# The stores of x in the attention, issued by SyncE behind a step's loads instead of by ScalarE

## The chip, the cores and the metric

The kernel runs on one core of one Trainium2 chip. The metric is the device time of one execution in microseconds. A core has five engines that run side by side, each with an instruction queue of its own: TensorE (PE; its weight loads are shown as PEld), VectorE (DVE), ScalarE (ACT), GpSimd (POOL) and SyncE (SP), which here only issues DMAs and waits. DMAs can be issued from the queues of SyncE, ScalarE and GpSimd, and are carried out by 16 DMA engines of the core.

## The reference

A recurrent attention block (4 batches, 8 heads, 768 positions, head size 48) is followed by a mixture of 8 experts, in which every expert gets exactly 384 of the 3072 rows.

```python
f = 1.0 / (1.0 + np.exp(-f_logit))
for t in range(S):
    state = f[:, :, t, :, None] * state + np.einsum('bhd,bhe->bhde', k[:, :, t], v[:, :, t])
    y[:, :, t] = np.einsum('bhd,bhde->bhe', q[:, :, t], state)
x = y.transpose(0, 2, 1, 3).reshape(B * S, H * D)          # 3072 x 384
logits = x @ w_gate                                        # 3072 x 8
# the best free (row, expert) pair first; every expert takes N / E = 384 rows: assigned[row]
for e in range(E):
    out[assigned == e] = np.maximum(x[assigned == e] @ w1[e], 0.0) @ w2[e]
```

## The kernel before

The attention is cut into 24 chunks: 6 stretches of 128 positions for each of the 4 batches, all 8 heads of a chunk at once. A chunk passes through stages, and the stages of several chunks are run beside each other: in step s, the stage with number n works on chunk s - n. There are 29 steps. The order of the stages in a step is written out by hand (lists `FILLING` for the first 6 steps, `FULL`, `LAST`), and the scheduler keeps that order on TensorE, VectorE, ScalarE and GpSimd. SyncE is not in that list: the order of its DMAs is the scheduler's, which takes them as it expects them to become possible.

What happens to a chunk, with the names that the text uses:

- `load` (L169, SyncE): f of the chunk three steps ahead, then q, k and v of the chunk two steps ahead, at the head of each step. Each is 192 KB, read as 1024 runs of 192 bytes. f has three buffers, q and k four, v seven; a load waits until its buffer's last reader is done.
- `clamp` (L175, GpSimd), the last but two in a step, on the chunk of the next step; `decays` (L180, L181, ScalarE): exp and log of f give g.
- `split` (L191 VectorE `upper`, L193 GpSimd `low`, L199 ScalarE `high`), then `sums` (L210, TensorE): running sums L of g.
- `factors` (L221 VectorE `dl`, L223 and L224 ScalarE `eq`, `ek`), and q and k times these: `gated_q` (L240), `gated_k` (L246, GpSimd).
- `halves` and `span` (L235, L250, L254 GpSimd, L256 ScalarE `gl`), `decayed` (L289, GpSimd R), `added` (L299) and `new_state` (L311): the state that goes on to the batch's next chunk.
- `q_columns` and `k_columns` (L264 TensorE, L272 ScalarE `qT`, L279 VectorE `kT`): transposes.
- `scores` (L322 TensorE A, L327 VectorE `am`), `values` (L337) and `queries` (L351): the chunk's rows of x in PSUM (Y). In `queries` ScalarE copies them to the tile x in SBUF (L358, two copies) and, before the change, issues the store of x to `xd` in HBM (L361). x has three buffers.
- `transposed` (L370, TensorE X), `x_copy` (L382, VectorE), `gate` (L390), `to_logits` (L400): the logits of the chunk, from the x in SBUF.

In a step of `FULL`, `queries` (stage 4) is the last but one: ScalarE copies and stores the x of chunk s - 4 at the step's end, and the first thing in its queue behind that is `decays` of the next step. TensorE starts the next step with `transposed` of the same x. The scratch array `xd` is read much later: the gather of an expert's rows (L1034, GpSimd) takes rows of it by number.

After the attention the experts' rows are found by counting, and expert after expert is computed, while the next expert's rows are found.

Every DMA that SyncE or ScalarE issues counts up one of eight completion semaphores, which are handed round in the order that the scheduler gives the DMAs; before one is used again, the issuing engine waits until the DMA that had it before has landed. That wait is an instruction in the issuing engine's queue.

Of the kernel before, what the change touches and what calls it, by code (L numbers as in the profile page):

```python
# [27 lines left out]
def kernel(  # L28
# [32 lines left out]
    nc = tc.nc  # L61
# [5 lines left out]
    C = 128  # L67
# [31 lines left out]
    xd = dram.tile([N + 32, D], FP32, name="xd")  # L99
# [243 lines left out]
    def queries(G):  # L343
        b, c, Y = G["b"], G["c"], G["Y"]
        G["x"] = x = work.tile([128, D], FP32, name="x", tag="x", bufs=3)
        if G["R"] is not None:
            for hp in range(HP):
                for j in range(2):
                    for par in range(2):
                        rows = slice(DP * par, DP * par + DH)  # L350
                        nc.tensor.matmul(  # L351
                            out=Y[par][HC * j:HC * j + HC, DH * hp:DH * hp + DH],
                            lhsT=G["qT"][rows, hp, HC * j:HC * j + HC],
                            rhs=G["R"][rows, hp, :],
                            start=False, stop=True, skip_group_check=True)
        for par in range(2):
            copy = nc.vector.tensor_copy if par and last(G) else nc.scalar.copy
            copy(out=x[:].rearrange("t (a r d) -> t r a d", r=2, d=DH)[:, par],  # L358
                 in_=Y[par][:, 0:HP * DH].rearrange("t (a d) -> t a d", d=DH))
        row = S * b + C * c  # L360
        nc.scalar.dma_start(out=xd[row:row + C, :], in_=x[:])  # L361

    def last(G):
        return G.get("i") == len(chunks) - 1
# [41 lines left out]
    def beside(G):  # L406
# [11 lines left out]
                        (added, 2), (values, 4), (halves, 1), (gate, 5), (gated_q, 1),  # L418
                        (new_state, 2), (decays, 0), (gated_k, 1), (span, 1), (to_logits, 5),
                        (split, 0), (beside, 0), (clamp, -1), (queries, 4), (split_high, 0),  # L420
                        (scores, 3)))
    FULL = ((decayed, 2), (decays, 0), (transposed, 5), (sums, 1), (added, 2), (x_copy, 5),
            (factors, 1), (split, 0), (split_high, 0), (k_copy, 3), (halves, 1), (new_state, 2),
            (values, 4), (span, 1), (gate, 5), (gated_q, 1), (gated_k, 1), (to_logits, 5),
            (q_columns, 2), (k_columns, 2), (k_last, 2), (beside, 0), (clamp, -1), (queries, 4),
            (scores, 3))
    LAST = ((scores, 3),) + FIRST + ((x_copy, 5), (k_copy, 2), (values, 4), (queries, 4),
                                     (gate, 5), (to_logits, 5), (counts_so_far, 5),
                                     (beside, 5))
# [59 lines left out]
    def ramp(n, name, step, base, when=later):  # L489
# [18 lines left out]
          in_=in_group[:].unsqueeze(2).to_broadcast((128, CG, E)))  # L508
# [813 lines left out]
    with tc.If(again[0] > 0):  # L1322
# [9 lines left out]
        with tc.For_i(0, B, 1) as b:  # L1332
            x = pool.tile([128, NCH, D], FP32, name="xb", tag="xb", bufs=1)
            with tc.For_i(0, HP, 1) as hp:
                scan_pair(pool, x, b, hp)
            nc.sync.dma_start(
                out=xd[0:N, :].rearrange("(b c t) d -> b t c d", b=B, c=NCH)[
                    bass.ds(b, 1)].rearrange("b t c d -> (b t) c d"),
                in_=x[:])
# [12 lines left out]
        out=outs[NT - 1][:, :],  # L1352
        out_offset=bass.IndirectOffsetOnAxis(ap=last_token[:, TE - 1:TE], axis=0),
        in_=o[:], in_offset=None, bounds_check=N - 1, oob_is_err=False)
# [29 lines left out]
```

## Time and profile before

| | |
|---|---|
| median of 9 runs | 452.08 us (449.57 to 454.69) |
| the profiled execution | 451.56 us |
| its span, first to last instruction | 449.6 us |
| granted TensorE clock, mean | 0.977 of full speed |
| TensorE busy | 428.4 us, 95% |
| VectorE busy | 274.5 us, 61% |
| ScalarE busy | 128.7 us, 29% |
| GpSimd busy | 175.1 us, 39% |
| loads of f, q, k and v | 24 each, 192 KB, 5.1, 4.5, 4.8 and 4.8 us from issue to landing (medians) |
| stores of x | 24, 192 KB, 3.1 us from issue to landing, first at 23.8 us, last at 151.9 us |
| DMA queue q10 | 3504 packets, 4.77 MB, 3.0% of the span of 16 engines |

In the lines of the profile, L361 is line 361 of the kernel, `out<-in` are the kernel's names of tiles, and "x24" is a count. In a timeline the first column is the start in microseconds from the first instruction, the second the length; what stands in brackets is how long the engine had been idle before, and what ended that. ACTq and SPq are the sequencers of ScalarE and SyncE, where a DMA's issue shows. The rows of 40 digits give the busy share in tenths for 40 equal slices of the span.

### The profile page before, as it was taken

The page shows a single profiled execution, that of the slowest core. Times are in us where ns is not written, and L with a number is a line of the kernel's source. Part 1 is how long each engine was busy: PE and PEld are TensorE (multiplying, and loading weights), DVE is VectorE, ACT ScalarE, POOL GpSimd, SP SyncE. Part 2 cuts the span into 40 slices and gives each one's busy share as a digit, 9 for nine tenths or more (in the row PEclk, how much of TensorE's full clock was granted, in tenths as well). Part 3 has the DMA queues.
Part 4 walks back from the last instruction along what each step waited for, and adds up shares of the span by engine and source line. Part 5 has one row for each costly group of instructions (what it writes and reads, how often), then busy time and mean ns, then how long its engine had stood idle before and what let it go on. Part 6 is the DMA issues. An engine that isn't in the chain of part 4 may idle for free. (4 is left out here: it accounts for less than half of the span.)

```text
span 449.6 us, 11815 instructions
## 1 busy us (share of the span) xinstructions
PE 428.4 (95%) x4830; PEld 288.3 (64%) x4830; DVE 274.5 (61%) x879; ACT 128.7 (29%) x302; POOL 175.1 (39%) x231
## 2 busy tenths in 40 slices
PE   8999999999999759999999999999999999999994
PEld 5788887888888635565555555565565565555552
DVE  5788877778987686677667666667667662000000
ACT  4666655666562001210210210210210211211210
POOL 2466545666551012036137037047046046531001
PEclk9999999999999958999999999999999999999998
DMA  9999888999611109074193183083183187710001
GB/s 158 179 206 200 187 186 174 208 201 181 139 39 43 50 9 327 1 273 128 42 331 88 24 329 88 22 330 88 30 322 88 28 324 230 245 38 35 1 19 39
DMA packets 135200, 63.25 MB, mean 141 GB/s; under 512 B 118464, under 2 KB 129760, under 8 KB 135136
## 3 DMA queue, kind: packets, MB, share of 16 engines
q1 hardware_dynamic: 128560, 48.19, 43.8%
q0 software_dynamic: 3072, 9.44, 5.9%
q10 hardware_dynamic: 3504, 4.77, 3.0%
q8 instruction: 40, 0.66, 0.6%
q14 instruction: 24, 0.20, 0.1%
HBM read 48.77 MB, written 9.49 MB: 130 GB/s over the span
## 5 line engine op out<-in xcount | busy, mean ns | idle before, releaser
L1103 PE MATMUL H<-xeT,w 128*128 128x384 f32 x384 | 132.7, 495 | 0.1
L1103 PEld LDWEIGHTS H<-xeT,w 128*128 128x128 f32 x384 | 69.4, 190 | 43.5 <-issue 4.5
L1115 PE MATMUL O<-w,hT 128*128 128x384 f32 x192 | 66.1, 492 | 0.0
L1115 PE MATMUL last_O<-w,hT 128*128 128x384 f32 x192 | 65.9, 492 | 0.0
L1107 ACT ACTIVATE hT<-H 128x384 f32<-128x384 f32 x64 | 31.4, 490 | 104.4 <-PE H L1103 103.0
L1115 PEld LDWEIGHTS last_O<-w,hT 128*128 128x128 f32 x192 | 35.3, 190 | 23.6 <-issue 2.2
L1115 PEld LDWEIGHTS O<-w,hT 128*128 128x128 f32 x192 | 35.2, 190 | 23.5 <-issue 2.3
L327 DVE COPY_PREDICATED am<-mask,A 128x512 f32<-128x512 int32 x48 | 32.4, 729 | 14.6 <-PE A L322 14.6
L193 POOL TENSOR_TENSOR low<-g,upper 128x384 fp32r<-128x384 f32 x22 | 22.2, 1011 | 45.0 <-DVE upper L191 35.9
L992 POOL TENSOR_TENSOR block<-past 128x72 f32<-128x72 f32 x8 | 2.4, 304 | 84.5 <-DVE at L569 73.2
L1034 POOL DMA_INDIRECT xe<-xd,token x21 | 21.3, 1014 | 26.1 <-DVE full L566 15.9
L1120 POOL DMA_INDIRECT out_dram<-o,token x21 | 21.4, 1017 | 21.3 <-ACT o L1119 18.4
L337 PE MATMUL Y<-v,am 128*64 128x48 f32 x768 | 27.4, 223 | 0.6 <-DVE am L327 0.6
L1072 POOL COPY xeT<-cols 128x768 uint16<-128x768 uint16 x21 | 22.3, 1064 | 12.8 <-DMA cols<-parts 12.8
L322 PE MATMUL A<-qT,kT 48*64 48x128 f32 x768 | 26.2, 272 | 0.6 <-issue 0.6
L246 POOL TENSOR_TENSOR kg<-k,ek 128x384 f32<-128x384 f32 x23 | 23.1, 1004 | 8.0 <-ACT ek L224 8.0
L337 PEld LDWEIGHTS Y<-v,am 128*64 128x64 f32 x768 | 24.8, 138 | 1.5 <-DVE am L327 1.0
L1062 POOL COPY parts<-xe 128x768 uint16<-128x768 uint16 x21 | 17.7, 876 | 15.9 <-DMA xe<-xd,token 14.1
L1119 ACT COPY o<-O 128x384 f32<-128x384 f32 x12 | 5.7, 478 | 59.9 <-PE O L1115 54.7
L322 PEld LDWEIGHTS A<-qT,kT 48*64 48x64 f32 x768 | 21.1, 133 | 1.2 <-issue 1.1
L128 PE MATMUL nothing<-idle,ones 128*128 128x384 bf16 x74 | 19.7, 406 | 1.6 <-DVE ones L133 1.5
L1119 ACT COPY o<-last_O 128x384 f32<-128x384 f32 x11 | 5.3, 478 | 54.0 <-PE last_O L1115 48.8
(230 smaller groups left out, 677.6 us busy)
## 6 DMA issues: line engine op xcount, KB each, us to landing
w<-in_moe_w_dram SPq DMA_DIRECT2D x16, 1536.0 KB, 8.6
f<-in_f_logit_dram SPq DMA_DIRECT2D x24, 192.0 KB, 5.1
q<-in_q_dram SPq DMA_DIRECT2D x24, 192.0 KB, 4.5
k<-in_k_dram SPq DMA_DIRECT2D x24, 192.0 KB, 4.8
v<-in_v_dram SPq DMA_DIRECT2D x24, 192.0 KB, 4.8
xd<-x ACTq DMA_DIRECT2D x24, 192.0 KB, 3.1
xe<-xd,token POOLq DMA_INDIRECT x21
cols<-parts SPq DMA_TRANSPOSE x21, 2.8
```

The lines of the kernel that those rows point to most:

```text
L128: nc.tensor.matmul(out=nothing[:, 0:CAP], lhsT=ones[:], rhs=idle[:], start=True, stop=True)
L193: nc.gpsimd.tensor_tensor(out=low[:], in0=g[:, :, 0:DH], in1=upper[:].bitcast(FP32), op=ALU.subtract)
L246: engine.tensor_tensor(out=G["kg"][:, :, 0:DH], in0=G["k"][:], in1=G["ek"][:], op=ALU.mult)
L322: nc.tensor.matmul(out=A[par][HC * j:HC * j + HC, 128 * hp:128 * hp + 128], lhsT=G["kT"][rows, hp, HC * j:HC * j + HC], rhs=G["qT"][rows, ...
L327: nc.vector.copy_predicated(am[:, par], mask[:].unsqueeze(1).to_broadcast((128, HP, 128)), A[par][:].rearrange("s (a t) -> s a t", t=128))
L337: nc.tensor.matmul(out=Y[par][HC * j:HC * j + HC, DH * hp:DH * hp + DH], lhsT=G["am"][:, par, hp, HC * j:HC * j + HC], rhs=G["v"][:, 2 * h ...
L1034: nc.gpsimd.indirect_dma_start(out=xe[:], out_offset=None, in_=xd[:, :], in_offset=bass.IndirectOffsetOnAxis(ap=token[:, i:i + 1], axis=0))
L1072: nc.gpsimd.tensor_copy(out=halves[:, :, :, 128 * i:128 * i + 128], in_=t[:].rearrange("p (h c) t -> p h c t", h=2))
L1103: nc.tensor.matmul(out=L["H"][:, 0:CAP], lhsT=L["w1"][:, d, 128 * ft:128 * ft + 128], rhs=xT[:, d, :], start=(d == 0), stop=(d == DC - 1))
L1107: nc.scalar.activation(out=hT[:, ft, :], in_=L["H"][:, 0:CAP], func=AF.Relu)
L1115: nc.tensor.matmul(out=L["O"][:, 0:D], lhsT=hT[:, ft, 128 * i:128 * i + 128], rhs=L["w2"][:, ft, :], start=(ft == 0), stop=(ft == FC - 1))
L1120: nc.gpsimd.indirect_dma_start(out=outs[next(tiles)][:, :], out_offset=bass.IndirectOffsetOnAxis(ap=L["token"][:, i:i + 1], axis=0), in_=o ...
```

## The change

The store of a chunk's x to `xd` is issued from SyncE's queue instead of ScalarE's. In the program's order it stands behind the loads of its step. The transfer itself, 128 rows of 1536 bytes, is the same. The store of zeros behind the last row of `xd` (L464) stays with ScalarE.

```diff
         row = S * b + C * c
-        nc.scalar.dma_start(out=xd[row:row + C, :], in_=x[:])
+
+        nc.sync.dma_start(out=xd[row:row + C, :], in_=x[:])
```

## The prediction

> **What bounds the kernel now.** I read the page first, to find the stage that the change touches, then the timelines of ScalarE, TensorE and SyncE in it.
>
> ```profile
> PE   8999999999999759999999999999999999999994
> ...
> ACT  4666655666562001210210210210210211211210
> ...
> DMA  9999888999611109074193183083183187710001
> ```
>
> A slice is 11.24 us. The stores stand in the first fourteen (23.8 to 151.9 us). There TensorE is full, ScalarE about 60% busy, and the DMA engines are full until the last load, near slice 10. So a store that costs only ScalarE's time would be free; what matters is whom it holds up.
>
> ```profile
> 51.13 0.54 ACT L358 COPY x<-Y 128x192 f32<-128x192 f32 x2
> 52.63 0.34 ACTq L361 DMA_DIRECT2D xd<-x  x1
> 53.02 0.52 ACT L180 ACTIVATE f<-f 128x384 f32<-128x384 f32 x1 [1.35 <-DMA f<-in_f_logit_dram]
> ...
> 56.80 0.54 ACT L358 COPY x<-Y 128x192 f32<-128x192 f32 x2
> 59.37 0.38 ACTq L361 DMA_DIRECT2D xd<-x  x1
> 59.79 0.52 ACT L180 ACTIVATE f<-f 128x384 f32<-128x384 f32 x1 [2.45 <-DMA q<-in_q_dram]
> ```
>
> This is ScalarE's timeline. The x that the store at 59.37 sends is ready at 57.34, so the store itself stood for 2.0 us, and the decays (L180) stood behind it. What ended the wait is the landing of a q load, which neither of them reads. The built program says why: every DMA of SyncE and ScalarE waits for one of eight completion semaphores, handed round in the scheduler's order, and a store can only go when the load that held its semaphore before has landed. The idle times that this puts before the decays, from 52.6 to 88.0 us, are 1.35, 2.45, 1.69, 2.27, 1.52, 0.78 and 0.64 us: 10.7 us in seven steps. TensorE's timeline shows how much of it arrives:
>
> ```profile
> 57.65 0.55 PE L370 MATMUL X<-ident,x 128*128 128x128 f32 x3
> ...
> 62.31 1.07 PE L322 MATMUL A<-qT,kT 48*64 48x128 f32 x32
> 64.09 0.55 PE L370 MATMUL X<-ident,x 128*128 128x128 f32 x3 [0.71 <-ACT x L358]
> ```
>
> The late decays make `upper` late (VectorE waits 0.89 us for ScalarE's g before 60.90), then `low` and `gl` on GpSimd, then `gl`, `qT` and the x copy on ScalarE, and X waits for x. The first transposes of X start at 51.90, 57.65, 64.09, 70.03, 76.55, 82.32, 87.99, 93.66 and 99.33: steps of 5.75, 6.44, 5.94, 6.52, 5.77, 5.67, 5.67 and 5.67. A step in which TensorE waits for nothing is 5.67 us.
>
> **The change, part by part.** *Removed from ScalarE: 24 issues and their waits.* The waits cost TensorE what the five long steps have above 5.67: 0.08 + 0.77 + 0.27 + 0.85 + 0.10 = 2.07 us. They go, because no other DMA is left in ScalarE's queue but the one of zeros at 14.6. What is late next is TensorE itself, as in the steps after 82 us. The issues are 24 x 0.34 = 8.2 us; in the steady steps ScalarE idles about 1.1 us before `eq` (for `dl`, VectorE) and 0.55 us before `gl`, which hides them, so nothing. Without that cover it would be the 8.2 us. Only in the step at 29 us does TensorE wait for `high`, which stands behind a store of 0.40: 0.34 us there, of which I take 0.2 (filler matmuls stand beside it).
>
> *Added to SyncE: 24 issues, behind a step's loads.* SyncE's order in the changed program is f, q, k, v, store for most steps, and in steps from the 16th on up to two loads pass the store. Each store waits for ScalarE's x copy, for its semaphore and for room in the queue; behind it stand the loads of the next step. Who waits for those: `clamp` on GpSimd for f two steps later, and the gates for q and k. Is SyncE free enough?
>
> ```profile
> 30.88 1.19 SPq L169 DMA_DIRECT2D v<-in_v_dram  x1
> 32.16 0.73 SPq L169 DMA_DIRECT2D f<-in_f_logit_dram  x1
> 32.98 2.19 SPq L169 DMA_DIRECT2D q<-in_q_dram  x1
> ...
> 54.81 2.79 SPq L169 DMA_DIRECT2D k<-in_k_dram  x1
> ```
>
> This is SyncE's timeline: it issues with hardly a pause, and an issue lasts 0.37 to 3.31 us, 0.8 to 0.9 in the middle. From 27.80 (f of chunk 7) to 102.61 (v of chunk 21) it issues 60 loads in 74.8 us, 1.25 each, 4.99 for the four of a step. With a store it needs 4.99 + X, and 0.09 for a gap. The step allows 5.67, so X may be 0.59. Bounds for X: below, the 0.34 of ScalarE's issue; above, a load's mean of 1.25. I take 0.45: the 4.99 already holds the transfers of the stores, which run on the same engines before and after, and queue q10, which carries only the stores, took 3.0% of the span, 13.5 us over 25, 0.54 each, about half of a load's 1.0 at the start of SyncE's timeline. Then SyncE needs 5.5 us of 5.67, and the added cost is nothing.
>
> *Moved: when x lands.* x has three buffers, so the store of chunk 0 must land before the copy of chunk 3 at 39.96. Its place on SyncE is behind the v at 30.88, so it goes at 32.1 instead of 23.82.
>
> ```profile
> L361 ACTq DMA_DIRECT2D xd<-x x24: 338/339/403, 23.8 to 151.9; - x24
> ...
> DMA to landing us min/median/max: 1.9/3.1/5.1
> ```
>
> By these rows of the tile x a store lands 3.1 us after its issue in ScalarE's queue; a load in SyncE's takes 4.5 to 5.1 (the page's list of issues). Taking 5.1 the store lands at 37.2, a cover of 2.8 us. The f of chunk 8, issued at 32.16, lands at 37.0 for a clamp at 40.28, 3.3 us. Both hold as long as SyncE keeps the step's pace. If that cover is gone, each step pays what SyncE takes above 5.67. The last store (151.92) is read by the gather at 169.85, 15 us later, so a slower landing there is free, as is the load of the first expert's number behind it, which waits for VectorE until about 165.7.
>
> The Trainium skill's page "DMA: Bandwidth & Descriptors", section "Queues, rings and completion order", speaks against the move: each DMA engine goes round between the queue rows packet by packet, so a store in ScalarE's row gets its turn beside the loads, and in SyncE's row it stands behind them. The 3.1 against 4.5 to 5.1 agrees, and the sum has it in the cover of 2.8. The same page, "Issuing engines are not separate DMA queues", says that spreading issues over engines saves only sequencer time; by it alone the change would move 8.2 us of issue between two sequencers off the path and be worth 0. The rows above say that it also takes away a wait.
>
> The sum: -2.07 - 0.2 = -2.3 us. The profiled execution took 451.56 us, 1.96 more than its span of 449.6, and would take 449.3. It stands 0.5 below the median of the nine runs, 452.08, so I forecast 449.8 for the median, 0.5% below. Differences under about 0.5% (2.26 us) can't be told from none in this kernel; its nine runs lie between 449.57 and 454.69.
>
> **The rivals.**
>
> *Larger gain.* What TensorE sees is the tip of 10.7 us; the first 1.0 to 1.5 us of each wait vanish in ScalarE's idle time. Landings a little later than in this profile count in full: 0.3 us more in each of seven waits is 2.1, so 447.7. For it: the median run is slower than the profiled one. Against: nothing shows that this is why.
>
> *Slower: SyncE becomes the bound of the attention.* Sixteen stores stand between loads. With X above 0.59 SyncE falls behind by X - 0.59 a step until 2.8 us are used up, and the rest is paid: 16(X - 0.59) - 2.8. At X = 0.77 nothing is paid yet, at 0.90 the loss of 2.2 eats the gain, and from 1.05 the kernel is slower by over 0.5%. At a load's mean, 1.25, the loss is 7.8: 449.8 + 7.8 = 457.6. For it: SyncE has little to spare, and its issues last up to 3.31 us. Against: a store is 128 rows of 1.5 KB, a load 1024 runs of 192 B.
>
> *Nothing.* The copy of x waits for landings instead of the store for a semaphore, or the gain falls under TensorE's own limit: 451.5 to 452.5.
>
> **How the numbers follow.** The forecast has 0.60. Its middle lies on the bound of 0.5%, so I split it 0.34 faster and 0.26 same (its own range 448.7 to 450.9). Larger gain 0.15, slower 0.17, nothing 0.08. Faster 0.34 + 0.15 = 0.49, same 0.26 + 0.08 = 0.34, slower 0.17. The range, 447.4 to 454.6, takes in the larger gain, the forecast and nothing, and the slower case up to X of about 1.05.
>
> **What the profile after would show.** Right: the decays start within 0.2 us of the x copy's end in every step from 50 to 90 us; the starts of X stand 5.67 apart there; the stores on SyncE issue in 0.34 to 0.6 us, some 7 us after their x in the early steps; 2 us less at the last X (151.98). Wrong: x copies that wait for a DMA's landing, `clamp` waiting for f, or X steps of 5.9 and more after 60 us (SyncE is the bound); or X steps as long as before with another releaser.

## The result, and the profile after

The changed kernel takes 449.26 us (median of 20 runs, 448.07 to 449.96) beside 451.92 us (62 runs, 449.13 to 456.89) of the kernel before: a ratio of 0.9938, with a 95% interval of 0.9923 to 0.9952. A second set of runs, later, gave 449.13 beside 450.69: 0.9965 (0.9948 to 0.9981). So the change brings 1.6 to 2.7 us. A few executions of these kernels are slower throughout (up to 475 us); the ratios leave them out, and so do the medians of "delays on ScalarE" and "two buffers of x" below. The profiled execution took 449.29 us, its span is 447.2 (before 451.56 and 449.6).

The page of the changed kernel:

```profile
ACT  4666665666652101210210210210210211211210
...
DMA  9989988888941118084193083183183087720001
...
q1 hardware_dynamic: 132016, 52.91, 46.9%
...
q10 hardware_dynamic: 48, 0.05, 0.0%
...
xd<-x SPq DMA_DIRECT2D x24, 192.0 KB, 4.1
```

Queue q10 is left with the DMA of zeros, and the stores' 3456 packets are in q1. The busy rows hardly move: what the change does can't be seen there. ScalarE's timeline shows it:

```profile
50.74 0.54 ACT L358 COPY x<-Y 128x192 f32<-128x192 f32 x2
51.57 0.53 ACT L180 ACTIVATE f<-f 128x384 f32<-128x384 f32 x1 [0.29 <-POOL f L175]
...
56.42 0.54 ACT L358 COPY x<-Y 128x192 f32<-128x192 f32 x2
57.25 0.53 ACT L180 ACTIVATE f<-f 128x384 f32<-128x384 f32 x1 [0.30 <-POOL f L175]
```

These are the places where the kernel before had the store and 1.35 and 2.45 us of idle time that the landing of a load ended. Now 0.29 and 0.30 us are left, and the clamp on GpSimd ends them. From 50 to 84 us no wait of ScalarE ends with a DMA any more; before there were five of 9.3 us together. What SyncE does instead, in its timeline, and the group of the stores under the tile x:

```profile
57.56 0.85 SPq L169 DMA_DIRECT2D v<-in_v_dram  x1
58.50 2.90 SPq L362 DMA_DIRECT2D xd<-x  x1
61.49 0.39 SPq L169 DMA_DIRECT2D f<-in_f_logit_dram  x1
```

```profile
L362 SPq DMA_DIRECT2D xd<-x x24: 332/899/2897, 32.8 to 150.0; - x24
...
DMA to landing us min/median/max: 1.9/4.1/5.4
```

A store's issue lasts 0.90 us in the median, not 0.34 (338 ns) as on ScalarE, and it starts 7 to 9 us behind its x in the early steps. Nobody waits for that: no x copy waits for a store to land, and the clamp never waits for f behind the start.

The starts of X stand 5.67 apart from 51.52 to 97.77 in all steps but two, of 6.08 and 6.15. From the first X to the last it is 125.54 us, before 127.29: 1.75 of the span's 2.4. The first X is 0.17 earlier. Behind the attention 0.4 more differs. There the profiles of this study scatter: from the last X to the end of the span it is 297.56 to 298.61 in the six with the stores on ScalarE, and 297.05 to 297.80 in seven with the stores on SyncE (all but that of two buffers). The two ranges overlap, so whether the change saves something there too is not shown.

In the two long steps TensorE stood, and no other engine had kept it waiting. The second of them:

```profile
70.72 1.11 PE L337 MATMUL Y<-v,am 128*64 128x48 f32 x31
72.06 0.26 PE L337 MATMUL Y<-v,am 128*64 128x48 f32 x1 [0.23 <-issue]
```

The 32nd matmul of one group of `values` starts half a microsecond late. The experiments come back to what that is.

### The profile page after: what moved, and what is told of

The parts are those of the page before. It is cut to its first block, busy times and chain, and to the rows that moved or that the text cites. A ratio compares the mean times of both kernels' runs of the same rounds, so it can differ in the third digit from the quotient of the medians.

```text
span 447.2 us, 11817 instructions
## 1 busy us (share of the span) xinstructions
PE 427.1 (96%) x4830; PEld 287.9 (64%) x4830; DVE 273.0 (61%) x879; ACT 129.2 (29%) x302; POOL 174.5 (39%) x231
## 5 line engine op out<-in xcount | busy, mean ns | idle before, releaser
L223 ACT ACTIVATE eq<-dl 128x384 f32<-128x384 f32 x24 | 12.6, 523 | 32.3 <-DVE dl L221 32.3
```

## The experiments

Times are medians; "before" is the kernel before in the same set of runs. The ratios are not quotients of these medians and can differ from them by 0.2%. The last column is from the first X to the last in the profile, that is, the attention without what lies around it.

| kernel | stores issued by | us | before, us | ratio (95%) | first X to last X |
|---|---|---|---|---|---|
| before | ScalarE | 451.92 | | | 127.29 |
| before, again | ScalarE | 450.95 | 450.96 | 1.0001 (0.9976 to 1.0026) | 125.25 |
| changed | SyncE | 449.26 | 451.92 | 0.9938 (0.9923 to 0.9952) | 125.54 |
| changed, again | SyncE | 449.13 | 450.69 | 0.9965 (0.9948 to 0.9981) | 124.64 |
| behind the decays | ScalarE | 450.78 | 450.70 | 1.0024 (0.9999 to 1.0050) | 126.67 |
| behind the decays, again | ScalarE | 450.84 | 450.96 | 0.9990 (0.9966 to 1.0015) | 127.21 |
| behind `high` | ScalarE | 451.17 | 450.96 | 1.0001 (0.9978 to 1.0024) | 125.95 |
| behind the decays, less q | ScalarE | 449.37 | 450.96 | 0.9963 (0.9940 to 0.9986) | 124.63 |
| ScalarE's time alone | SyncE | 449.41 | 450.70 | 0.9983 (0.9965 to 1.0002) | 125.52 |
| a small DMA on ScalarE | SyncE | 449.54 | 450.70 | 0.9978 (0.9959 to 0.9996) | 125.84 |
| delays on ScalarE | SyncE | 455.69 | 450.69 | 1.0113 (1.0083 to 1.0143) | 131.12 |
| stores twice | SyncE | 449.10 | 450.69 | 0.9974 (0.9953 to 0.9995) | 124.67 |
| stores late | SyncE | 450.09 | 450.69 | 0.9991 (0.9973 to 1.0010) | 124.57 |
| two buffers of x | SyncE | 451.34 | 450.70 | 1.0033 (1.0006 to 1.0060) | |

**Was it ScalarE's time?**

```diff
+        nc.scalar.copy(out=dummy[:], in_=x[:, 0:192])
         nc.sync.dma_start(out=xd[row:row + C, :], in_=x[:])
```

> The changed kernel, and in the store's old place ScalarE makes a copy of half of x into a tile that nobody reads, about 0.3 us, as long as the issue that was taken away and without its wait. Theory (the wait): the decays now wait 0.28 to 0.30 us for the clamp anyway, which hides it: 449.0 to 449.6 us. Rival, issue time: the gain is gone, 451.9 us.

449.41 us, and 125.52 from the first X to the last, as the changed kernel's first profile. Work as long as the 24 issues costs ScalarE nothing here: from 50 to 100 us the decays start about 0.3 us behind the x copy's end in all steps but one, with the extra copy or without it, since the clamp ends there. (Each of the two profiles has two of TensorE's stops in it, so the equal 125.5 is partly chance.)

**Did the changed kernel's second execution look the same?**

> The changed kernel once more, as the measure for the other kernels beside it, and for a second profile of it. Theory of the wait: 449.3 us, ratio 0.994, decays 0.3 us behind the x copy in every step, the first X to the last 125.5 us (before 127.3). Theory of the instruction fetch (TensorE stops where its next 16 KB of instructions have not landed, 1.3 to 1.5 us after such a fetch ends): stops of 0.3 to 0.5 us again, in other steps than in the first profile, 0 to 2 us of them in all.

The time held; the attention was 0.9 us shorter, at 124.64, with every step from 52.28 to 97.64 of 5.67 us. None of TensorE's stops was there. So they are not part of the program's order, but come and go.

**And the kernel before?** It was run once more for a second profile.

> The kernel before, for a second profile. Theory of the wait: the decays stand 1 to 2.7 us behind the x copies from 50 to 80 us again, the first X to the last takes 126.5 to 127.5 us (the changed kernel: 125.5 and 124.6), as the store waits for the same loads in every execution. Rival (the first profile was an accident): 125.5 us or less.

A miss on the size. The decays stood 0.60, 0.50, 1.15, 1.48, 1.86 and 0.53 us behind the x copies in the six steps from 52 to 81 us, and only that of 1.86 reached TensorE, in a step of 5.99 (0.32 above 5.67). A step of 5.81 there is not the wait's: its decays were 0.50 us behind. The first X to the last took 125.25. The wait is there in both executions, but what TensorE sees of it went from 2.07 to 0.32 us between two executions of one program.

**How much of a delay reaches TensorE?**

```diff
+        for _ in range({5: 5, 6: 10, 7: 6, 8: 9, 9: 6}.get(G["i"], 0)):
+            nc.scalar.copy(out=dummy[:], in_=x[:, 0:192])
         nc.sync.dma_start(out=xd[row:row + C, :], in_=x[:])
```

> The changed kernel, and behind the x copies of chunks 5 to 9 ScalarE makes 5, 10, 6, 9 and 6 copies of 0.27 us into a tile that nobody reads: 1.35, 2.7, 1.62, 2.43 and 1.62 us, as long as the decays stood behind the x copy in the kernel before (1.35, 2.67, 1.69, 2.49, 1.52). All else is as after the change. Theory of the wait, by the prediction's term: TensorE gives back 2.07 us, in the same five steps, so 2.0 us above the changed kernel beside it. With the instruction fetch: a TensorE that is held up does not run out of instructions there, so 1.0 to 2.0 us. Rival, the queues (only the transfers' order matters): no difference from the changed kernel.

The copies took longer than set, about 0.37 us each, as the delay of chunk 6 in ScalarE's timeline shows, and the gap it makes in TensorE's:

```profile
57.39 3.82 ACT L364 COPY dummy<-x 128x192 f32<-128x192 f32 x10
61.11 0.52 ACT L182 ACTIVATE f<-f 128x384 f32<-128x384 f32 x1
```

```profile
63.33 1.10 PE L324 MATMUL A<-qT,kT 48*64 48x128 f32 x32 [1.07 <-DVE kT L281]
65.41 0.55 PE L374 MATMUL X<-ident,x 128*128 128x128 f32 x3 [0.98 <-ACT x L360]
```

The decays stood 1.83, 3.76, 2.22, 3.37 and 2.21 us behind the x copies, and the five steps were 5.91, 8.00, 6.47, 7.62 and 6.47: 0.24, 2.33, 0.80, 1.95 and 0.80 above 5.67, 6.1 in all. The time rose by 6.6 us over the changed kernel's. So the rival that only the order of transfers counts falls: ScalarE's lateness by itself does it. The first 1.4 to 1.6 us of each delay vanish here (1.3 to 1.7 in the first profile of before), the rest arrives in full. (The 2.67 and 2.49 us of the expectation are counted from the end of the first of the two x copies; from the end of both they are 2.45 and 2.27.) That is why the kernel before can lose 2.07 us in one execution and 0.32 in another: its delays of 0.5 to 2.45 us lie on both sides of that edge.

**Does the wait come back with a DMA on ScalarE?**

```diff
+        nc.scalar.dma_start(out=xs[G["i"]:G["i"] + 1, :], in_=x[0:1, 0:128])
         nc.sync.dma_start(out=xd[row:row + C, :], in_=x[:])
```

> The changed kernel, and in the store's old place ScalarE issues a DMA of one row of 512 bytes, into an array that nobody reads. So the wait and the issue are back on ScalarE, the bytes stay in SyncE's queue. Theory (the wait): the gain is gone, and as SyncE's loads now stand behind stores too, their semaphores may come free later: 451.5 to 453.5 us. Rival, issue time: 451.9. Rival, the queues: 449.3.

The wait came back, the loss in the median hardly: 449.54, beside 449.41 for the kernel with the extra copy. ScalarE's timeline has it at its longest:

```profile
99.43 0.22 ACTq L362 DMA_DIRECT2D xs<-x  x1
99.70 0.52 ACT L181 ACTIVATE f<-f 128x384 f32<-128x384 f32 x1 [2.55 <-DMA v<-in_v_dram]
```

It cost that step 0.81 us (6.62, where the changed kernel has 5.81); two more steps lost 0.26 and 0.10, and this execution, at 450.17, is 0.6 above its median. All other waits were under 1.9 us, below or near the edge. With six DMAs a step in place of five the eight semaphores come round in another order, so other loads had held them; that this is why the waits were short is argued and not shown. My 451.5 to 453.5 took the waits to be as long as before, and they were not.

**Elsewhere on ScalarE.** If the decays are all that matters, the store can stay on ScalarE behind them (as a stage `store` of its own; the lists `FILLING` and `LAST` get it too):

```diff
-    FULL = ((decayed, 2), (decays, 0), (transposed, 5), (sums, 1), (added, 2), (x_copy, 5),
+    FULL = ((decayed, 2), (decays, 0), (store, 5), (transposed, 5), (sums, 1), (added, 2), (x_copy, 5),
```

> The stores stay on ScalarE, but each is issued behind the decays of the next step instead of ahead of them. Theory (the decays stood behind the store's wait for a semaphore): the stores still wait, up to 2 us behind their x, but the decays have used about 1.1 us of that and ScalarE idles 1.2 us before eq, so little arrives at TensorE: 449 to 450.2 us, most of the change's gain. Rival, ScalarE's issue time (24 x 0.34 us that ScalarE no longer spends): 451.9, as the issues are the same. Rival, the queues (the loads land earlier because the stores stand in SyncE's row): 451.9, as the stores are still in ScalarE's row.

> The stores on ScalarE behind the decays, a second time, for a second profile and beside other kernels. In the first its decays started 0.3 us behind the x copies, as after the change, but TensorE stopped five times for its instructions, 2.0 us in all from 50 to 106 us. Theory (a store in ScalarE's queue runs beside the loads and makes fetches later): such stops again, 1 to 2.5 us, and 450.5 to 451 us. Rival (the stops fall by chance in any kernel, 0.9 and 0 us in two profiles of the changed one): 0 to 0.9 us of stops and 449.3 us.

The same behind `split_high`, ahead of `gl`:

> The stores on ScalarE, each some 2 us later still, behind the next step's split_high. The decays stand free, as in the kernel beside it. Theory (stores in ScalarE's queue make fetches later): stops of 1 to 2.5 us from 50 to 106 us, 450.5 to 451 us. Rival (chance): 449.3 us. If a store's wait now holds up gl and qT on ScalarE, the steps are longer with ScalarE as the releaser, not with TensorE stopped 1.3 to 1.5 us behind a fetch.

All three runs give the time of the kernel before: my theory, in the form that the place ahead of the decays is to blame, fell. The profiles show two losses in place of the one. In the second, ScalarE's timeline has the store's wait ahead of `eq`, and with the store behind `high` it stands ahead of `gl` in step after step:

```profile
73.74 0.52 ACT L223 ACTIVATE eq<-dl 128x384 f32<-128x384 f32 x1 [3.12 <-DMA v<-in_v_dram]
```

```profile
57.06 0.21 ACT L256 ACTIVATE gl<-gl 128x4 f32<-128x4 f32 x1 [1.05 <-DMA f<-in_f_logit_dram]
...
62.79 0.21 ACT L256 ACTIVATE gl<-gl 128x4 f32<-128x4 f32 x1 [1.11 <-DMA q<-in_q_dram]
...
68.74 0.20 ACT L256 ACTIVATE gl<-gl 128x4 f32<-128x4 f32 x1 [1.08 <-DMA k<-in_k_dram]
```

In the first no wait of ScalarE from 50 to 84 us ends with a DMA, and yet the attention is 2.0 us longer than the changed kernel's second. There it is TensorE that stops, as at 72.06 above, five times:

```profile
91.60 0.66 PE L351 MATMUL Y<-R,qT 48*64 48x48 f32 x27
92.42 0.26 PE L351 MATMUL Y<-R,qT 48*64 48x48 f32 x3 [0.15 <-issue]
```

Counting TensorE's instructions (matmuls and weight loads) in the trace from 0, this stop is before number 4033, those beside it before 3777 and 4289, that at 72.06 before 3009. In all profiles together there are 17 stops of 0.2 us and more, in eight profiles, that no engine explains while the loads run, and all stand before a number 256n + 193. And queue q8, which carries instructions in blocks of 16384 bytes, always ended such a block 1.3 to 1.5 us earlier (at 70.69 for the stop at 72.06, at 91.14 for that at 92.42). From 25 to 107 us the fourteen profiles have 233 passages of such a number, and none comes sooner than 1.27 us after the end of a block. So I read the stops thus: TensorE had used up one block of instructions, and the next had only just come. The Trainium skill's page "Runtime: NRT & Kernel Launch", section "Instruction fetch mechanics", says that an engine fetches its instructions in blocks of 16 KiB, 256 instructions, which is the spacing seen; it calls the cost of crossing a block mostly hidden, and here it was 0 to 2 us in an attention.

**Is it the traffic?** The same kernel with an eighth of the loads gone:

```diff
+            if nm == "q" and G["i"] % 2:
+                G[nm] = chunks[G["i"] - 1][nm]
+                continue
```

> The stores on ScalarE behind the decays, and q is loaded for every second chunk only (the odd chunks take the q of the chunk before, so the values are others; the instructions of the four compute engines are the same). An eighth of the loads is gone. Theory of the instruction fetch (fetches are late because the DMA engines are full): no stops from 50 to 106 us, steps of 5.67, 449 to 449.5 us, as the changed kernel. Rival (the loss comes from where the stores are issued, whatever the traffic): 450.5 to 451 us.

449.37 us and 124.63 from the first X to the last: all steps 5.67 from 51.88 to 97.24, no stop, though the stores are issued by ScalarE. From 50 to 106 us the DMA engines were 75 to 83% busy here, 85 to 95% in the first profile of the same kernel with all loads. So with an eighth of the loads gone the place of the stores does not matter. That it is the fullness of the DMA engines is not shown: there are also fewer DMAs to share the eight semaphores, and fewer issues on SyncE.

**The rival with SyncE as the bound.**

```diff
         nc.sync.dma_start(out=xd[row:row + C, :], in_=x[:])
+        nc.sync.dma_start(out=xd2[row:row + C, :], in_=x[:])
```

> The changed kernel, and SyncE stores every x a second time, into an array that nobody reads. The prediction's rival by its formula: SyncE needed 5.30 us a step with one store up to 77 us, 0.90 of it the store, so 6.2 to 6.4 with two, 0.5 to 0.75 above the step's 5.67; 16 x that, less the 2.8 of cover, is 5.7 to 9.2 us: 455 to 458.5 us, with x copies that wait for a DMA. If SyncE is not close to its limit: 449.3 to 450 us.

No loss at all: 449.10 us, 124.67. SyncE's timeline shows why:

```profile
66.15 0.76 SPq L363 DMA_DIRECT2D xd<-x  x1
66.96 0.42 SPq L364 DMA_DIRECT2D xd<-x  x1
67.47 0.42 SPq L170 DMA_DIRECT2D f<-in_f_logit_dram  x1
```

The second store's issue takes 0.42 us. From the f of chunk 8 at 32.69 to that of chunk 21 at 105.93 SyncE takes 5.63 us a step with two stores, 5.53 with one (34.44 to 106.34), 5.36 and 5.22 with none (the two profiles of before). The second store added 0.1 us to the step, or 0.3 if four loads are counted as a step (5.63 beside 5.33), which is less than its own issue's length: the issues are long where SyncE is held back, and one DMA more takes the place of some of that time instead of adding to it.

**Two buffers of x instead of three:**

```diff
-        G["x"] = x = work.tile([128, D], FP32, name="x", tag="x", bufs=3)
+        G["x"] = x = work.tile([128, D], FP32, name="x", tag="x", bufs=2)
```

> The changed kernel with two buffers of x instead of three. The prediction's step on the landing of x: the store of chunk 0 lands at 36.7, and x is now wanted again at about 34.3 instead of 39.6, so the copy waits some 2.4 us; SyncE needs 5.3 to 5.5 us a step, so it falls no further behind and the loss is paid once: 451 to 452.5 us. Rival (SyncE falls behind in every step): over 455. Rival (the lateness of the stores does not matter): 449.3.

451.34 us, 1.93 above the kernel with ScalarE's extra copy in the same set. ScalarE's timeline has the wait for the landing of the first store:

```profile
34.35 0.57 ACT L272 COPY qT<-T 128x512 f32<-128x512 f32 x1
36.67 0.54 ACT L358 COPY x<-Y 128x192 f32<-128x192 f32 x2 [1.76 <-DMA xd<-x]
```

1.76 us, 2.4 expected. (TensorE's granted clock is 0.50 from 38 to 47 us in this profile, so its later steps are not used, and that the wait comes only once is read from the time alone.) The cover that three buffers give is real.

**All stores held back:**

```diff
-        nc.sync.dma_start(out=xd[row:row + C, :], in_=x[:])
+        held.append((S * b + C * c, x))
...
+            for _ in range(min(len(held), 0 if step < 15 else 3)):
+                row, x = held.popleft()
+                nc.sync.dma_start(out=xd[row:row + C, :], in_=x[:])
```

> The changed kernel with 14 buffers of x and the stores held back: SyncE issues none before the loads of the first 15 chunks, then up to three a step. Theory of the instruction fetch (it is late because the DMA engines are full of loads and stores): with a fifth of the traffic gone from 30 to 100 us TensorE stops less, the steps are 5.67 throughout there, and the kernel is 0.3 to 1 us below the changed kernel beside it. Theory of the wait alone: the same time as the changed kernel, as ScalarE issues nothing in either.

The first store went out at 71.6, when SyncE had the loads of 15 chunks behind it. The profiled execution has no stop and 124.57 from the first X to the last, the least of all. But the median, 450.09, is 0.96 above the changed kernel's; the profiled execution is the quickest of its twelve (448.69), so it does not show what the others lose. So holding the stores back gains nothing; why stays open.

## Why the prediction was right, and where not

The forecast, 449.8 us and slightly faster, was met at 449.3. By its steps:

- *The waits removed, −2.07, and 0.2 in the step at 29 us.* Right in kind, and in that execution in size: by the X starts the long steps are gone, and the first steps gave 0.22. As a size for the median it was one draw: the second profile of before lost only 0.32 to the wait. Between the two second profiles (450.27 and 449.04) the attention differs by 0.62, of which 0.32 is the wait and 0.15 the first steps, and 1.0 lies behind the last X. So what the wait has of the median's gain is not settled, and that the sum came so near was in part luck. Of a delay TensorE does not see the first 1.4 to 1.6 us by the kernel with delays, where I had 1.0 to 1.5. That the decays start within 0.2 us was not met: 0.30, since the clamp ends there. It costs nothing.
- *What is late next is TensorE itself.* This step failed. In the first profile of after TensorE's instructions were late twice, 0.41 and 0.48 us, so −2.3 became −1.4 up to there; −1.75 from the first X to the last it is only because the kernel before has a stop of the same kind later, 0.8 us before number 5313 in its step of 6.65 at 117 us, of which 0.35 is left at the last X.
- *24 issues for nothing.* Shown by the kernel with ScalarE's time alone, where the clamp covers 0.3 us of each step.
- *SyncE needs 4.99 + X.* The total was near (5.5 forecast, 5.53 measured), the terms were wrong: X was 0.90, twice my 0.45, and the loads' issues shrank (f from a median of 0.78 us to 0.39). A sum of issue lengths is no demand while the queue holds the issuer back. So the loss of 2.2 us which the slower rival's formula gives at X = 0.90 did not come, nor the 5.7 to 9.2 with two stores.
- *When x lands.* Store of chunk 0 issued at 32.81 (forecast 32.1), landed 36.73 (37.2), wanted 39.58: a cover of 2.85 us (2.8). With two buffers the wait came, as the step says. The store's later turn in SyncE's row was not steady: 4.1 us to landing in the first profile, 3.3 in the second, 3.1 and 3.0 before.
- *The rule of the Trainium skill's page "DMA: Bandwidth & Descriptors", section "Issuing engines are not separate DMA queues", that spreading issues over engines saves only the sequencer's time,* would have given 0. Measured were −1.6 and −2.7 us. The rule leaves out what stands ahead of the issue: a wait for a semaphore that another engine's load holds.
- *Larger gain.* The first pairing of medians lies 2.66 apart, the second 1.56: the forecast's 2.3 lies between, and neither decides for this rival.

What stays open: whether a store in ScalarE's queue makes TensorE's fetches later, or only leaves less room for their lateness. Up to 107 us all three profiles with the store elsewhere on ScalarE and all loads have stops (five, two and one), the two of before have none, and of those with the stores on SyncE, apart from that of two buffers, three have two each and four none. That is too few for a cause.

## What to carry to other kernels

What a DMA issued by a compute engine cost that engine here was not its issue but what the issue waits for, and that can be another engine's load which it has nothing to do with; look at what ended the idle time behind it, and move such issues to an engine that only issues. Before adding to an issuing engine, ask whether its issues are long because the queue holds them back: if so, their sum overstates what one more costs. And take a second profile before trusting the size of a wait that depends on landings.

## What the runs showed of the hardware

- The 17 stops of TensorE stand at boundaries of 256 instructions, and it goes on 1.3 to 1.5 us behind the end of a fetch. The fetches last 0.9 to 2.0 us, and 94% of those for the 233 passages begin 20 to 200 instructions behind the boundary before, so a late one leaves little of the block's 256.
- In the changed kernel, from 44 to 77 us, each of the seven issues of SyncE that last over 1.4 us (1.68 to 2.90) has the start of an instruction fetch inside it, whatever it loads or stores; the others last 0.37 to 1.22. Elsewhere the link is loose: of the 178 issues of loads and stores on SyncE over 1.4 us from 30 to 105 us in the fourteen profiles, 98 have one.
- An issue on SyncE right behind a store is short: 0.37 to 0.43 us for most f and for the second store, where the first store, behind a v, has a median of 0.76.
